# Two decoder layers over a cached grouped-query attention: the first layer's kept heads in another order, a two-head softmax in other steps, and V products issued ahead of scores

## The chip, the cores and the metric

The kernel runs on one core of one Trainium2 chip. The metric is the device time of one execution in microseconds (us), the median of the runs shown. One execution was also taken by the hardware profiler; all lines of profile below come from that one.

## What is computed

Two layers, each an attention block over a long cache and a dense block, one token for each of 8 batches. Both layers read the same caches.

```python
# B=8, one query, D=512, Hq=32, Hkv=8, Sk=8192, Dh=128, F=1792, all bf16
q = (x @ wq) as 32 heads of 128
scores = einsum("bhqd,bhkd->bhqk", q, repeat(k_cache, 4)) * 128**-0.5
o = einsum("bhqk,bhkd->bhqd", softmax(scores), repeat(v_cache, 4)) @ wo

x = x + attention(layernorm(x)); x = x + silu_mlp(layernorm(x))
x = x + attention(layernorm(x)); x = x + silu_mlp(layernorm(x))
```

The K cache and the V cache have 134 MB each, so that two layers that read everything anew would move 537 MB. Four query heads share one K/V head.

## The kernel before

**Tasks and positions.** A task is one layer, batch and K/V head: 128 tasks, in an order that `make_tasks` fixes. A task has 8 positions (`GPT`), two for each of its 4 granules. A granule is 2048 keys of one head: 512 KB, one slot of the ring `ARENA`, which has 28 slots. The build is one loop over positions p; what it emits at each p, in the order of the loop's body, is the order in which every engine runs its part, since each engine runs its list in order.

**Kept heads.** `KEEP = 20` granules, the five heads 3 to 7 of a batch, stay in the ring between the two layers, so that their K is read once for both. Heads 0 to 2 are read twice. V is read in both layers. For each batch the first layer's five kept heads follow each other; then come tasks of heads 0 to 2 of either layer; then the second layer's kept heads. `READ` says how many granules one K load of a kept head brings: 4 for each, a whole head, 2 MB in one transfer. Heads 4 and 5, and 6 and 7 (`DUOS`), are pairs: their rows are interleaved in the ring, they share one softmax, and their V comes in transfers of two granules (1 MB).

**Loads.** `plan_loads` gives each load the position that needs it (`need`), a slot, and the position after which this slot is free (`after`). All loads go through SP's queue in order of `need` (`issue_until`, L394); a load waits there for the last reader of its slot, and those behind it wait too.

**Steps of a task** with first position p0. (1) `emit_t` (L516, DVE): each K granule is transposed in place, one position ahead. (2) `emit_s` (PE): scores. A solo head's granule is L606 with 128 columns, a whole solo head L606 with 512, a whole head of a pair L578 (`score_both`). A whole head in layer one is scored at its last position, p0+7. (3) `softmax`, two tasks later, by phases `p % 8`, for a pair at the positions of its first head's turn: phase 0 maxima (L620, L626 on DVE, L629 on POOL), 2 shift and first exponential (L635 and L638 on DVE, L642 on ACT), 3 first head's transposition on PE (L667) and second exponential, 4 row sums (L655 on DVE for a pair, L652 on ACT for a solo head; then L658 on POOL), 5 last transposition (L667) and copies to `PT` (L674, ACT), 7 reciprocal (L681, DVE). The exponentials use one buffer `P`, so that the second waits for the first one's transposition. (4) `emit_pv` (L711, PE) runs 22 positions (`LP`) behind the scores: a pair's two granules at once, on every fourth position. (5) `emit_own` (L728, ACT), `emit_join` (L736, DVE), `emit_fold` (L750, PE) and `emit_norm` (L760, DVE) bring the head's output into `at`; one position later PE multiplies it by its part of `wo` (L873).

In the loop's body at one position the order is: transposes, scores, V products, own, join, fold, softmax phase, `wo` part or a piece of the dense block's chain, norm, loads.

Of the kernel before, what the change touches and what calls it, by code (L numbers as in the profile page):

```python
# [15 lines left out]
GPT = 8  # L16
GPG = 2
NSLOT = 28
SCORED = 2
READ = (1, 1, 1, 4, 4, 4, 4, 4)  # L20
DUOS = (4, 6)
KEEP = 20
LT = 1
PRE = 10
# [120 lines left out]
class Load:  # L145


    __slots__ = ("kind", "b", "g", "k", "turn", "need", "free", "slot", "after", "wide")

    def __init__(self, kind, b, g, k, need, free, wide=1):  # L150
        self.kind, self.b, self.g, self.k, self.turn = kind, b, g, k, k
        self.need, self.free, self.wide = need, free, wide
        self.slot, self.after = None, None

# [9 lines left out]
def make_tasks(nb, nkv, keep_from):  # L164


    first = int(keep_from)
    a = [[(0, b, g) for g in range(first)] for b in range(nb)]
    kept = [[(0, b, g) for g in range(first, nkv)] for b in range(nb)]
    c = [[(1, b, g) for g in range(first, nkv)] for b in range(nb)]  # L170
    d = [[(1, b, g) for g in range(first)] for b in range(nb)]
    ahead = [t for b in range(1, nb) for t in a[b]]
    behind = []
    tasks = a[0] + kept[0]
    na = gone = 0

    def whole(line, n):
        return n == len(line) or lead_of(line[n][2]) == line[n][2]

    for b in range(nb):  # L180
        if b:
            tasks += kept[b]
        if b == nb - 1:
            nd, nt = len(behind), len(ahead) - na
        else:
            due = 2 * first * (nb - 1) * (b + 1) / nb
            must = first * (b + 1)
# [12 lines left out]


def plan_loads(tasks, kept, nslot, ngran):

    at = {t: i for i, t in enumerate(tasks)}
    loads = []
    for i, (layer, b, g) in enumerate(tasks):
        for k in range(ngran):
            i0 = i * GPT + k * GPG
            if layer == 0 and (g, k) in kept:
                w = READ[g]  # L210
                if k % w == 0:
                    loads.append(Load("K", b, g, k, -1 if i0 < PRE else i0 - LT,
                                      at[(1, b, g)] * GPT + SCORED * GPG + GPG - 1, w))
            elif (g, k) not in kept:
                loads.append(Load("K", b, g, k, -1 if i0 < PRE else i0 - LT, i * GPT + (k + 1) * GPG - 1))
            w = members(g)
            if k % w == 0:
                loads.append(Load("V", b, g, k, i0 + GPG - 1 + LP, i0 + GPG - 1 + LP, w))
    loads.sort(key=lambda d: (d.need, d.kind == "K" and d.wide == 1))
    free = {s: -2 for s in range(nslot)}  # L220
# [42 lines left out]
def _build(ctx, nc, A_x, A_k_cache, A_v_cache, A_wq, A_wo, B_w1, B_w2, out):  # L263
# [43 lines left out]
    def half(slot, h):  # L307
# [29 lines left out]
              "eps": 1, "shift": 1, "eh": FT, "vr": 1, "yr": 1, "tr": 1, "s1": 1, "s1a": 1, "s2": 1, "s2a": 1,  # L337
              "top": DR, "tops": DR, "ssm": DR, "xn": KT // 2, "hs": FT // 2}
    widths.update({f"ssa{n}": DR for n in range(NST)})
    widths.update({f"rs{n}": 2 for n in range(NST)})  # L340
# [69 lines left out]
    t_slot = {}  # L410
    v_slot = {}

    def issue(d):
        cache = A_k_cache if d.kind == "K" else A_v_cache
        own, lead, n = d.g - lead_of(d.g), lead_of(d.g), members(d.g)
        if d.kind == "K":
            rows = cache[d.b, lead:lead + n].rearrange("g (p f) d -> (g p) (f d)", p=128 // n)
            at = own if d.wide > 1 else d.k * n + own
            src = rows[:, at * d.wide * SLOT:(at + 1) * d.wide * SLOT]
        else:  # L420
            src = cache[d.b, d.g].rearrange("(k p c) d -> k p (c d)", k=NGRAN // n, p=128)[d.k // n]
        dst = ARENA[:, d.slot * SLOT:(d.slot + d.wide) * SLOT]
# [6 lines left out]
    with nc.Block() as block:  # L429

        @block.sync
        def _(sync_eng):
# [136 lines left out]

            def score_both(ti, slots, qn):  # L570
                own = tasks[ti][2] - lead_of(tasks[ti][2])
                cols = NGRAN // 2 * 128
                many = ARENA[:, slots[0] * SLOT:(slots[0] + NGRAN) * SLOT].rearrange(
                    "p (k u t x h j e) -> p u t h e k x j", u=2, t=NQ, x=CPB, h=PAIRS, e=2, j=QUAD)
                for u in range(2):
                    bank = (ti - own + u) % NSCP
                    mm_group([
                        lambda n=n, t=t: pe.matmul(  # L578
                            SCp[bank][t * QUAD:t * QUAD + USED, own * cols:(own + 1) * cols], QB[qn][:, n, :],
                            many[:, u, t, n // 2, n % 2], start=(n == 0), stop=(n == NPART - 1))  # L580
                        for n in range(NPART) for t in range(NQ)
                    ], reads=[r_half(slot, h) for slot in slots for h in range(2)] + [f"QB{qn}"], writes=[f"SC{bank}"])

            def emit_s(i):
# [10 lines left out]
                if whole and members(g) > 1:  # L595
                    score_both(ti, slots, qn)
                    return
# [50 lines left out]
            def softmax_sum(ti):  # L648
                st, many = turn_of[ti] % NST, members(tasks[ti][2])
                w = many * REP  # L650
                if many == 1:
                    op(act, lambda: act.activation(ssm[:, 0:w], hm[:, :], ACT.Copy, scale=rs[st][:, 0:1]),  # L652
                       reads=["hm", f"rs{st}"], writes=["ssm"])
                else:
                    op(dve, lambda: dve.scalar_tensor_tensor(  # L655
                        ssm[:, 0:w], rs[st][:, 0:1].to_broadcast([128, w]), rs[st][:, 1:2], hm2, op0=ALU.add, op1=ALU.mult),
                       reads=["hm2", f"rs{st}"], writes=["ssm"])
                op(pool, lambda: pool.partition_all_reduce(ssa[st][:, 0:w], ssm[:, 0:w], 128, bass.bass_isa.ReduceOp.add),  # L658
                   reads=["ssm"], writes=[f"ssa{st}"])
# [19 lines left out]
            def softmax_rcp(ti):  # L679
                st, w = turn_of[ti] % NST, members(tasks[ti][2]) * REP  # L680
                op(dve, lambda: dve.reciprocal(ssa[st][:, 0:w], ssa[st][:, 0:w]), reads=[f"ssa{st}"], writes=[f"ssa{st}"])  # L681

            def softmax(ti, ph):
# [3 lines left out]
                elif ph == 2:  # L687
                    softmax_shift(ti)
                    softmax_exp(ti, 0)
                elif ph == 3 and many > 1:  # L690
                    emit_turn(ti, 0)
                    softmax_exp(ti, 1)
                elif ph == 4:
                    softmax_sum(ti)
                elif ph == 5:
                    emit_turn(ti, many - 1)
                    emit_pt(ti)
                elif ph == 7:
                    softmax_rcp(ti)

            def emit_pv(i):
                ti = i // GPT
                b, g, k, _h = where(i)
                if k % members(g):
                    return
                ob, own, many = ti % 2, g - lead_of(g), members(g)
                lead, at = ti - own, own * NGRAN // many + k // many
                w = XL if ti == ntask - 1 else XW
                parts = [(v_slot[(b, g, k + m)], (lead + m) % NPT) for m in range(many)]
                steps = [  # L710
# [4 lines left out]
                        start=(k == 0 and slot == parts[0][0] and y == 0),  # L715
                        stop=(k + many == NGRAN and slot == parts[-1][0] and y == CPB // w - 1),
                    )
# [35 lines left out]
            def emit_norm(ti):  # L753
                layer, b, g = tasks[ti]
                ob, st, own = ti % 2, turn_of[ti] % NST, g - lead_of(g)
                if layer == 0:
                    dst, rd = at1[b % NAT][:, g * REP:(g + 1) * REP], f"at1_{b % NAT}"
# [339 lines left out]

            kept_from = min(g for g, _k in kept)

            def calm(p):  # L1100
                if p >= NG:
                    return False
                return p >= task_at[(0, turn[0], kept_from)] * GPT

            for p in range(NG + LP + GPT + FOLD + 1):
# [7 lines left out]
                emit_t_until(p + LT)  # L1113
                if p % GPG == GPG - 1 and p < NG:
                    emit_s(p)
                if (p - LP) % GPG == GPG - 1 and 0 <= p - LP < NG:
                    emit_pv(p - LP)
                copied = p - LP - GPT
                if copied >= 0 and copied % GPT == 0 and copied // GPT < ntask:
# [5 lines left out]
                if folded >= 0 and folded % GPT == 0 and folded // GPT < ntask:  # L1125
                    emit_fold(folded // GPT)
                ti = p // GPT - 2
                if 0 <= ti < ntask and lead_of(tasks[ti][2]) == tasks[ti][2]:
                    softmax(ti, p % GPT)
                if chain:  # L1130
# [61 lines left out]
```

## Time and profile before

| what | value |
|---|---|
| median of 3 runs (lowest to highest) | 1168.55 us (1166.8 to 1169.06) |
| profiled execution: its own time, its span | 1169.76 us, 1168.0 us |
| busy: PE, DVE, ACT, POOL | 692.2, 738.9, 315.1, 90.7 us |
| read from memory | 465.05 MB, 398 GB/s over the span |
| mean granted TensorE clock | 0.62 of full speed |
| transposes L516 on DVE | 352, 430.1 us busy, mean 1231 ns |
| maxima L620 on DVE | 128, 86.3 us, mean 674 ns |
| exponentials L642 on ACT | 128, 180.8 us, mean 1413 ns |
| V products L711 on PE | 2064, 259.9 us |
| pair sums L655 on DVE | 32, 7.3 us busy; 88.7 us idle just before them, until ACT's L642 |
| K loads of 2 MB; V loads of 1 MB | 40; 128 |

The span is the time from the first to the last instruction, and the rest of the execution's time lies around it. An idle time belongs to the engine that waited, and the name behind the arrow is what ended the wait. DMA share is the mean busy share of the core's 16 DMA engines. A queue called SPq is SP's sequencer, which issues loads. A pair's task and a solo head's task take the same 8 positions.

### The profile page before, as it was taken

How to read it: one execution, taken by the hardware profiler on the slowest of the kernel's cores; microseconds unless marked ns; L12 is line 12 of the kernel's file. 1: busy time of each engine (PE TensorE's matmuls, PEld its weight loads, DVE VectorE, ACT ScalarE, POOL GpSimd, SP SyncE). 2: the span in 40 equal slices, each digit the busy share in tenths (PEclk: the TensorE clock that was granted, in tenths of full speed). 3: DMA queues.
4: the chain of work that ended last, by engine and by line, in shares of the span. 5: the costliest groups of instructions: out<-in, count | busy, mean ns of one | idle time of the engine just before them, and what ended most of it. 6: DMA issues, size and time to landing. Idle time of an engine off the chain costs nothing.

```text
span 1168.0 us, 28238 instructions
## 1 busy us (share of the span) xinstructions
PE 692.2 (59%) x11792; PEld 377.8 (32%) x11792; DVE 738.9 (63%) x1719; ACT 315.1 (27%) x700; POOL 90.7 (8%) x232
## 2 busy tenths in 40 slices
PE   1525566556665566466665575456765576466676
PEld 1212343234233243133332342234332343133343
DVE  3836655876387664777477655777467664777473
ACT  0342123222322223312222233213322233312322
POOL 0000010001000010001100010001100010001000
PEclk9855565556655575655666577655565555666665
DMA  9999999999999999999999999999999999999993
GB/s 361 404 401 399 408 402 426 417 389 408 401 419 383 399 407 421 422 373 410 412 422 413 395 407 424 420 387 402 412 423 412 391 405 419 423 393 409 412 411 147
DMA packets 94175, 466.90 MB, mean 400 GB/s; under 512 B 9936, under 2 KB 14048, under 8 KB 71904
## 3 DMA queue, kind: packets, MB, share of 16 engines
q1 hardware_dynamic: 94048, 465.10, 98.8%
q8 instruction: 93, 1.52, 0.5%
q14 instruction: 34, 0.28, 0.1%
HBM read 465.05 MB, written 0.01 MB: 398 GB/s over the span
## 4 chain that ended last, share of the span: by engine, by line
DMA 40%; PE 19%; DVE 17%; issue 12%; ACT 6%; SPq 3%; POOL 2%; DVEq 0%; ACTq 0%; POOLq 0%
DMA arena<-in_A_k_cache_dram 33%; DMA arena<-in_A_v_cache_dram 7%; DVE E L736 6%; PE OTp L711 6%; DVE arena L516 4%; ACT E L642 4%; DVE row L620 3%; PE SCp L578 3%; SPq L394 3%; PE TPp L667 2%; PE SCp L606 2%; PE MISC L855 2%; ACT PT L674 1%; PE MISC L873 1%; PE OTp L750 1%
## 5 line engine op out<-in xcount | busy, mean ns | idle before, releaser
L516 DVE STREAM_TRANSPOSE arena<-arena 128x1024 int32<-128x1024 int32 x352 | 430.1, 1231 | 120.0 <-DMA arena<-in_A_k_cache_dram 119.9
L642 ACT ACTIVATE E<-SCp,row 128x512 bf16<-128x512 f32 x128 | 180.8, 1413 | 538.1 <-DVE row L638 463.5
L711 PE MATMUL OTp<-arena,PT 128*16 128x512 bf16 (+1 forms) x2064 | 259.9, 560 | 50.9 <-DMA arena<-in_A_v_cache_dram 31.0
L736 DVE SCALAR_TENSOR_TENSOR E<-OTp,row,E 128x128 f32<-128x128 f32 x381 | 130.4, 342 | 115.3 <-ACT E L728 97.9
L606 PE MATMUL SCp<-arena,QB 128*16 128x128 bf16 (+1 forms) x3328 | 139.3, 314 | 101.6 <-DVE arena L516 87.0
L667 PE MATMUL TPp<-ident,E 128*128 128x128 bf16 x512 | 73.4, 293 | 121.1 <-ACT E L642 120.5
L578 PE MATMUL SCp<-arena,QB 128*16 128x256 bf16 x2048 | 114.0, 389 | 47.1 <-DVE arena L516 30.4
L606 PEld LDWEIGHTS SCp<-arena,QB 128*16 128x16 bf16 x3328 | 70.3, 110 | 173.5 <-DVE arena L516 138.8
L667 PEld LDWEIGHTS TPp<-ident,E 128*128 128x128 bf16 x512 | 41.6, 125 | 185.9 <-ACT E L642 164.2
L750 PE MATMUL OTp<-row,E 128*128 128x4 f32 x254 | 66.4, 332 | 47.3 <-DVE E L736 46.9
L750 PEld LDWEIGHTS OTp<-row,E 128*128 128x128 f32 x254 | 55.4, 272 | 115.6 <-DVE E L736 103.2
L578 PEld LDWEIGHTS SCp<-arena,QB 128*16 128x16 bf16 x2048 | 61.0, 117 | 97.1 <-DVE arena L516 46.1
L629 POOL PARTITION_ALL_REDUCE row<-row x96 | 36.0, 375 | 689.7 <-DVE row L626 575.1
L728 ACT ACTIVATE E<-OTp,row 128x128 f32<-128x128 f32 x127 | 47.4, 373 | 152.4 <-PE OTp L711 152.4
L620 DVE TENSOR_REDUCE row<-SCp 128x1 f32<-128x512 f32 x128 | 86.3, 674 | 2.8
L711 PEld LDWEIGHTS OTp<-arena,PT 128*16 128x16 bf16 (+1 forms) x2064 | 53.5, 107 | 84.7 <-DMA arena<-in_A_v_cache_dram 40.4
L873 PE MATMUL MISC<-at,wo 128*128 128x32 bf16 x1024 | 37.0, 186 | 56.4 <-DVE at L760 55.3
L674 ACT COPY PT<-TPp 128x256 bf16<-128x256 bf16 x128 | 44.3, 372 | 84.6 <-PE TPp L667 84.6
L658 POOL PARTITION_ALL_REDUCE row<-row x96 | 41.3, 431 | 297.5 <-ACT row L652 137.9
L655 DVE SCALAR_TENSOR_TENSOR row<-row 128x8 f32<-128x8 f32 x32 | 7.3, 229 | 88.7 <-ACT E L642 88.7
L873 PEld LDWEIGHTS MISC<-at,wo 128*128 128x128 bf16 x1024 | 32.6, 104 | 65.9 <-DVE at L760 58.8
L563 DVE TENSOR_TENSOR QB<-QSp,row 128x64 bf16<-128x64 f32 (+1 forms) x128 | 24.0, 194 | 15.7 <-PE QSp L547 14.6
(104 smaller groups left out, 385.5 us busy)
## 6 DMA issues: line engine op xcount, KB each, us to landing
arena<-in_A_v_cache_dram SPq DMA_DIRECT2D x256, 512.0 KB, 8.5
arena<-in_A_v_cache_dram SPq DMA_DIRECT2D x128, 1024.0 KB, 12.2
arena<-in_A_k_cache_dram SPq DMA_DIRECT2D x192, 512.0 KB, 8.1
arena<-in_A_k_cache_dram SPq DMA_DIRECT2D x40, 2048.0 KB, 16.1
wq<-in_A_wq_dram SPq DMA_DIRECT2D x1, 4096.0 KB, 17.3
wo<-in_A_wo_dram SPq DMA_DIRECT2D x1, 4096.0 KB, 33.3
w<-in_B_w_dram SPq DMA_DIRECT2D x2, 1792.0 KB, 24.8
E<-in_A_x_dram SPq DMA_DIRECT2D x1, 8.0 KB
```

The source lines that it names most:

```text
L516: op(dve, lambda: dve.transpose(words, words), reads=[r_half(slot, 0), r_half(slot, 1)], writes=[r_half(slot, 0), r_half(slot, 1)])
L578: lambda n=n, t=t: pe.matmul(SCp[bank][t * QUAD:t * QUAD + USED, own * cols:(own + 1) * cols], QB[qn][:, n, :], many[:, u, t, n // 2, n % ...
L606: lambda n=n, t=t: pe.matmul(SCp[bank][t * QUAD:t * QUAD + USED, lo * 128:(lo + len(slots)) * 128], QB[qn][:, n, :], keys(t, n), start=(n ...
L620: op(dve, lambda: dve.tensor_reduce(rowmax[:, n:n + 1], SCp[bank][:, :], AX.X, ALU.max), reads=[f"SC{bank}"], writes=["rowmax"])
L642: op(act, lambda: act.activation(P[:, :].rearrange("p (x j k) -> p k x j", x=CPB, k=NGRAN), SCp[bank][:, :].rearrange("p (k x j) -> p k x ...
L667: lambda c=c: pe.transpose(tpv[:, c, :], P[:, c * 128:(c + 1) * 128], ident[:, :])
L674: op(act, lambda: act.copy(PT[pb][:, :, :, :, :].rearrange("p a t x r -> p x t a r"), tpv.rearrange("p x (t q) -> p x t q", q=QUAD)[:, :, ...
L711: lambda t=t, y=y, slot=slot, pb=pb: pe.matmul(OTp[ob][t * QUAD:t * QUAD + w * REP, 0:w * DH], PT[pb][:, at, t, y * w:(y + 1) * w].rearran ...
L728: op(act, lambda: act.activation(joint, OTp[ob][:, 0:DH], ACT.Copy, scale=own_x[:, 0:1]), reads=[f"OT{ob}", "own_x"], writes=["P"])
L736: op(dve, lambda x=x: dve.scalar_tensor_tensor(joint, OTp[ob][:, x * DH:(x + 1) * DH], own_x[:, x:x + 1], joint, op0=ALU.mult, op1=ALU.add ...
L750: lambda: pe.matmul(OTp[ob][:, 0:REP], joint, hm[:, :], start=True, stop=True)
L873: lambda o=o, h=h: pe.matmul(MISC[:, o * w:(o + 1) * w], wo_sb[:, h, o * 128:(o + 1) * 128], rhs_of(h).to_broadcast([128, w]) if n == 1 el ...
```

## The change

Four edits.

- **Order.** The first layer's kept heads of a batch come as 4, 5, 6, 7, 3, where they came as 3, 4, 5, 6, 7. The second layer's order is as it was.
- **Halves.** `READ[3]` goes from 4 to 2: head 3 is loaded in two transfers of 1 MB and scored in two groups, at its positions 3 and 7.
- **Two-head softmax.** First transposition and second exponential move from phase 3 to 4, last transposition and `PT` copies from 5 to 6 (ahead of `emit_own` there), and the row sums from 4 to 7. One DVE operation on both heads becomes two on ACT, one for each head, POOL sums 16 columns where it summed 8, and DVE adds the two halves. The reciprocal, of solo heads too, is emitted with `emit_norm` of the task's first head, where it was in phase 7.
- **V products first.** At a position at which a kept head is scored, in either layer, the V products go ahead of the scores.

Beside these, `plan_loads` may split a pair's V load in two where fewer than 8 positions (`AMPLE`) lie between `after` and `need`. With this order there is no such load: the plan has 128 V loads of 1 MB and 256 of 512 KB before and after. K loads are 192 of 512 KB, 16 of 1 MB and 32 of 2 MB.

```diff
-READ = (1, 1, 1, 4, 4, 4, 4, 4)
+READ = (1, 1, 1, 2, 4, 4, 4, 4)
+AMPLE = 8
...
-    kept = [[(0, b, g) for g in range(first, nkv)] for b in range(nb)]
+    kept = [[(0, b, g) for g in range(first, nkv) if members(g) > 1] + [(0, b, g) for g in range(first, nkv) if members(g) == 1] for b in range(nb)]
...
 def plan_loads(tasks, kept, nslot, ngran):
+    apart = set()
+    while True:
+        loads = deal(tasks, kept, nslot, ngran, apart)
+        close = {d.key for d in loads if d.kind == "V" and d.wide > 1 and d.need - d.after < AMPLE}
+        if not close:
+            return loads
+        apart |= close
...
             def softmax_sum(ti):
...
-                if many == 1:
-                    op(act, lambda: act.activation(ssm[:, 0:w], hm[:, :], ACT.Copy, scale=rs[st][:, 0:1]),
-                       reads=["hm", f"rs{st}"], writes=["ssm"])
-                else:
-                    op(dve, lambda: dve.scalar_tensor_tensor(
-                        ssm[:, 0:w], rs[st][:, 0:1].to_broadcast([128, w]), rs[st][:, 1:2], hm2, op0=ALU.add, op1=ALU.mult),
-                       reads=["hm2", f"rs{st}"], writes=["ssm"])
-                op(pool, lambda: pool.partition_all_reduce(ssa[st][:, 0:w], ssm[:, 0:w], 128, bass.bass_isa.ReduceOp.add),
+                for n in range(many):
+                    op(act, lambda: act.activation(ssm[:, n * w:(n + 1) * w], masks[many][0], ACT.Copy, scale=rs[st][:, n:n + 1]),
+                       reads=["hm", "hm2", f"rs{st}"], writes=["ssm"])
+                op(pool, lambda: pool.partition_all_reduce(
+                    ssa[st][:, 0:many * w], ssm[:, 0:many * w], 128, bass.bass_isa.ReduceOp.add),
                    reads=["ssm"], writes=[f"ssa{st}"])
...
             def softmax_rcp(ti):
+                if many > 1:
+                    op(dve, lambda: dve.tensor_tensor(ssa[st][:, 0:w], ssa[st][:, 0:w], ssa[st][:, w:2 * w], ALU.add),
+                       reads=[f"ssa{st}"], writes=[f"ssa{st}"])
                 op(dve, lambda: dve.reciprocal(ssa[st][:, 0:w], ssa[st][:, 0:w]), reads=[f"ssa{st}"], writes=[f"ssa{st}"])
...
-                elif ph == 3 and many > 1:
+                elif ph == 4 and many > 1:
                     emit_turn(ti, 0)
                     softmax_exp(ti, 1)
                 elif ph == 4:
                     softmax_sum(ti)
-                elif ph == 5:
+                elif ph == 5 and many == 1 or ph == 6 and many > 1:
                     emit_turn(ti, many - 1)
                     emit_pt(ti)
-                elif ph == 7:
-                    softmax_rcp(ti)
+                elif ph == 7 and many > 1:
+                    softmax_sum(ti)
...
             def emit_norm(ti):
+                if not own:
+                    softmax_rcp(ti)
...
-                if p % GPG == GPG - 1 and p < NG:
+                scored = p % GPG == GPG - 1 and p < NG
+                behind = scored and (tasks[p // GPT][2], p % GPT // GPG) in kept
+                if scored and not behind:
                     emit_s(p)
                 if (p - LP) % GPG == GPG - 1 and 0 <= p - LP < NG:
                     emit_pv(p - LP)
+                if behind:
+                    emit_s(p)
+                probs = p // GPT - 2
+                due_now = 0 <= probs < ntask and lead_of(tasks[probs][2]) == tasks[probs][2]
+                if due_now and p % GPT == 6:
+                    softmax(probs, 6)
```

More of the change, by code (lines that the diff above doesn't have):

```diff
@@ L145 @@
 class Load:
-    __slots__ = ("kind", "b", "g", "k", "turn", "need", "free", "slot", "after", "wide")
+    __slots__ = ("kind", "b", "g", "k", "turn", "need", "free", "slot", "after", "wide", "key")
     def __init__(self, kind, b, g, k, need, free, wide=1):
@@ L152, in __init__ @@
         self.need, self.free, self.wide = need, free, wide
-        self.slot, self.after = None, None
+        self.slot, self.after, self.key = None, None, None
 def lead_of(g):
@@ L202, in plan_loads, with deal @@
 def plan_loads(tasks, kept, nslot, ngran):
+    apart = set()
[5 more added lines that the diff above has]
+        apart |= close
+def deal(tasks, kept, nslot, ngran, apart):
     at = {t: i for i, t in enumerate(tasks)}
@@ L215, in plan_loads @@
                 loads.append(Load("K", b, g, k, -1 if i0 < PRE else i0 - LT, i * GPT + (k + 1) * GPG - 1))
-            w = members(g)
+            key = (layer, b, g, k // members(g))
+            w = 1 if key in apart else members(g)
             if k % w == 0:
                 loads.append(Load("V", b, g, k, i0 + GPG - 1 + LP, i0 + GPG - 1 + LP, w))
+                loads[-1].key = key
     loads.sort(key=lambda d: (d.need, d.kind == "K" and d.wide == 1))
@@ L337, in _build @@
               "eps": 1, "shift": 1, "eh": FT, "vr": 1, "yr": 1, "tr": 1, "s1": 1, "s1a": 1, "s2": 1, "s2a": 1,
-              "top": DR, "tops": DR, "ssm": DR, "xn": KT // 2, "hs": FT // 2}
-    widths.update({f"ssa{n}": DR for n in range(NST)})
+              "top": DR, "tops": DR, "ssm": 2 * DR, "xn": KT // 2, "hs": FT // 2}
+    widths.update({f"ssa{n}": 2 * DR for n in range(NST)})
     widths.update({f"rs{n}": 2 for n in range(NST)})
@@ L411, in _build @@
     v_slot = {}
+    v_wide = {}
     def issue(d):
@@ L417, in issue @@
             rows = cache[d.b, lead:lead + n].rearrange("g (p f) d -> (g p) (f d)", p=128 // n)
-            at = own if d.wide > 1 else d.k * n + own
+            at = (own * NGRAN + d.k) // d.wide if d.wide > 1 else d.k * n + own
             src = rows[:, at * d.wide * SLOT:(at + 1) * d.wide * SLOT]
         else:
-            src = cache[d.b, d.g].rearrange("(k p c) d -> k p (c d)", k=NGRAN // n, p=128)[d.k // n]
+            rows = cache[d.b, d.g].rearrange("(k p c) d -> k p (c d)", k=NGRAN // n, p=128)[d.k // n]
+            src = rows[:, d.k % n * SLOT:(d.k % n + d.wide) * SLOT]
+            v_wide[(d.b, d.g, d.k)] = d.wide
         dst = ARENA[:, d.slot * SLOT:(d.slot + d.wide) * SLOT]
@@ L568, in emit_q, with score_both @@
                        reads=["QS", "own_q"], writes=[f"QB{n}"])
-            def score_both(ti, slots, qn):
+            def score_both(ti, slots, qn, first):
                 own = tasks[ti][2] - lead_of(tasks[ti][2])
-                cols = NGRAN // 2 * 128
-                many = ARENA[:, slots[0] * SLOT:(slots[0] + NGRAN) * SLOT].rearrange(
+                lo = (own * NGRAN + first) // 2 * 128
+                hi = lo + len(slots) // 2 * 128
+                many = ARENA[:, slots[0] * SLOT:(slots[0] + len(slots)) * SLOT].rearrange(
                     "p (k u t x h j e) -> p u t h e k x j", u=2, t=NQ, x=CPB, h=PAIRS, e=2, j=QUAD)
@@ L578, in score_both @@
                         lambda n=n, t=t: pe.matmul(
-                            SCp[bank][t * QUAD:t * QUAD + USED, own * cols:(own + 1) * cols], QB[qn][:, n, :],
+                            SCp[bank][t * QUAD:t * QUAD + USED, lo:hi], QB[qn][:, n, :],
                             many[:, u, t, n // 2, n % 2], start=(n == 0), stop=(n == NPART - 1))
@@ L595, in emit_s @@
                 if whole and members(g) > 1:
-                    score_both(ti, slots, qn)
+                    score_both(ti, slots, qn, first)
                     return
@@ L679, in softmax_rcp @@
             def softmax_rcp(ti):
-                st, w = turn_of[ti] % NST, members(tasks[ti][2]) * REP
+                st, many = turn_of[ti] % NST, members(tasks[ti][2])
+                w = many * REP
+                if many > 1:
+                    op(dve, lambda: dve.tensor_tensor(ssa[st][:, 0:w], ssa[st][:, 0:w], ssa[st][:, w:2 * w], ALU.add),
+                       reads=[f"ssa{st}"], writes=[f"ssa{st}"])
                 op(dve, lambda: dve.reciprocal(ssa[st][:, 0:w], ssa[st][:, 0:w]), reads=[f"ssa{st}"], writes=[f"ssa{st}"])
@@ L703, in emit_pv @@
                 b, g, k, _h = where(i)
-                if k % members(g):
+                if v_wide.get((b, g, k - k % members(g)), 1) > 1 and k % members(g):
                     return
@@ L708, in emit_pv @@
                 w = XL if ti == ntask - 1 else XW
-                parts = [(v_slot[(b, g, k + m)], (lead + m) % NPT) for m in range(many)]
+                parts = [(v_slot[(b, g, k + m)], (lead + (k + m) % many) % NPT) for m in range(v_wide[(b, g, k)])]
                 steps = [
@@ L715, in emit_pv @@
                         start=(k == 0 and slot == parts[0][0] and y == 0),
-                        stop=(k + many == NGRAN and slot == parts[-1][0] and y == CPB // w - 1),
+                        stop=(k + len(parts) == NGRAN and slot == parts[-1][0] and y == CPB // w - 1),
                     )
@@ L1096, in _ @@
             due_of = {t: p for p, t in due.items()}
-            kept_from = min(g for g, _k in kept)
+            kept_heads = {g for g, _k in kept}
             def calm(p):
@@ L1102, in calm @@
                     return False
-                return p >= task_at[(0, turn[0], kept_from)] * GPT
+                return p >= min(task_at[(0, turn[0], g)] for g in kept_heads) * GPT
             for p in range(NG + LP + GPT + FOLD + 1):
@@ L1126, in _ @@
                     emit_fold(folded // GPT)
-                ti = p // GPT - 2
-                if 0 <= ti < ntask and lead_of(tasks[ti][2]) == tasks[ti][2]:
-                    softmax(ti, p % GPT)
+                if due_now and p % GPT != 6:
+                    softmax(probs, p % GPT)
                 if chain:
```

## The prediction

> **What bounds the kernel now.** I read the page's DMA rows and chain first, then busy time by windows, then the timeline around one dip.
>
> ```profile
> DMA  9999999999999999999999999999999999999993
> q1 hardware_dynamic: 94048, 465.10, 98.8%
> DMA 40%; PE 19%; DVE 17%; issue 12%; ACT 6%; SPq 3%; POOL 2%; DVEq 0%; ACTq 0%; POOLq 0%
> ```
>
> The DMA engines are busy for 98.8% of the span, DVE for 63%. The change moves the same 465 MB, so only pauses of the DMA stream can be won. Where they are (columns: stretch, length, busy time of PE, PEld, DVE, ACT, POOL, granted clock, DMA share, GB/s):
>
> ```profile
> 420.00:500.00 80.00, 48.25 (x728) 24.58 (x720) 47.36 (x122) 23.89 (x49) 6.39 (x16) 0.65 1.02 418
> 260.00:290.00 30.00, 20.88 (x490) 13.83 (x491) 21.50 (x56) 8.97 (x28) 4.01 (x10) 0.57 1.03 408
> 499.80:514.80 15.00, 9.47 (x156) 4.86 (x148) 12.29 (x23) 2.60 (x4) 0.37 (x1) 0.61 0.96 362
> 514.80:529.80 15.00, 7.93 (x142) 3.97 (x142) 9.50 (x17) 1.89 (x6) 0.40 (x1) 0.50 1.00 385
> ```
>
> 418 and 408 GB/s are an unbroken stream of large and of small loads. In the 30 us after head 7's K has landed (499.8 us in batch 3) it falls to 362 and 385. The same view for the eight batches gives, for the two stretches of 15 us: 399+386, 394+386, 375+375, 362+385, 404+384, 387+387, 386+389, 401+391. Against 410, each loses 15 x (2 - sum/410): 1.3, 1.5, 2.6, 2.7, 1.2, 1.7, 1.7, 1.0, together 13.5 us. That is nearly all that this change can reach: 1.7 us a batch.
>
> Why the stream thins out, in batch 3 (start, duration, engine, line; in brackets the idle time before and what ended it):
>
> ```profile
> 499.81 1.25 DVE L516 STREAM_TRANSPOSE arena<-arena 128x1024 int32<-128x1024 int32 x1 [1.86 <-DMA arena<-in_A_k_cache_dram]
> 505.79 1.89 PE L578 MATMUL SCp<-arena,QB 128*16 128x256 bf16 x32 [1.01 <-DVE arena L516]
> 506.09 1.25 DVE L516 STREAM_TRANSPOSE arena<-arena 128x1024 int32<-128x1024 int32 x1 [0.35 <-DMA arena<-in_A_k_cache_dram]
> 507.26 1.08 DVE L736 SCALAR_TENSOR_TENSOR E<-OTp,row,E 128x128 f32<-128x128 f32 x3
> 508.26 1.47 DVE L620 TENSOR_REDUCE row<-SCp 128x1 f32<-128x512 f32 x2
> 509.04 3.96 SPq L394 DMA_DIRECT2D arena<-in_A_k_cache_dram  x2
> 511.26 0.12 DVE L760 TENSOR_TENSOR at<-OTp,row 128x4 bf16<-128x4 f32 x1
> 511.75 1.44 ACT L642 ACTIVATE E<-SCp,row 128x512 bf16<-128x512 f32 x1 [6.56 <-DVE row L638]
> 513.37 0.61 PE L667 MATMUL TPp<-ident,E 128*128 128x128 bf16 x4
> 515.44 0.23 DVE L655 SCALAR_TENSOR_TENSOR row<-row 128x8 f32<-128x8 f32 x1 [2.64 <-ACT E L642]
> 517.40 1.07 PE L711 MATMUL OTp<-arena,PT 128*16 128x512 bf16 x8
> 518.56 0.33 SPq L394 DMA_DIRECT2D arena<-in_A_v_cache_dram  x1
> 522.29 1.25 DVE L516 STREAM_TRANSPOSE arena<-arena 128x1024 int32<-128x1024 int32 x1 [1.94 <-DMA arena<-in_A_k_cache_dram]
> 527.67 1.25 DVE L516 STREAM_TRANSPOSE arena<-arena 128x1024 int32<-128x1024 int32 x1 [2.52 <-DMA arena<-in_A_k_cache_dram]
> ```
>
> Call T the landing of head 7 (499.8) and a unit 512 KB, which takes 1.25 us in an unbroken stream (506.09 is unit 5: 6.29/5). Four transposes and the score take T to T+7.9; maxima at T+8.5; exponentials, transpositions and copies bring the V product of head 6 at T+17.6, and only then is its slot free for head 7's V, issued T+18.8. The rows at 522.29 and 527.67 are units 17 and 21 of the stream: due 521.05 and 526.05, so 1.2 and 1.6 us late. Two issues came too late: one at 512.7 (the second of the row at 509.04, which waits for the second granule's score behind the `wo` part and L760) and the one at 518.56.
>
> **The change, part by part.** In both plans 20 units lie from head 7's K through head 7's V, the last of them freed by head 6's V product: the loop is as long as it was. What changes is what runs inside it.
>
> *Order and V first.* Before, the loads that went out only after T+8 were units 11 to 20; after, the plan frees the slots of units 5 to 12 before T+1 those of 13 to 16 by V products at T+3.6 and T+6.1, no longer behind head 7's score (1.9 us), and those of 17 and 18 by one at T+15. So the issue at T+12.9 and its followers are no longer late. Gain: at most the 1.2 us that unit 17 was late, 8 x 1.2 = 9.6 us.
>
> *The pair's chain gets longer.* Head 3's first half now stands where the single granule of 506.09 stood: its transpose is ahead of the join (L736) and the maxima on DVE, and 1 MB lands at unit 6 (T+7.5), not 5. Transpose 1.25 and join 1.08 put the maxima at T+9.8, 1.3 later. Then reciprocal (L681, 0.19) and the new add (as L623, 0.16) stand ahead of L760: +0.35, and the `wo` part waits for L760 as before. Behind it PE has the V product (1.06) and now a score of 2 granules (16 of L578's 32: 0.94, where L606 took 0.4 here) ahead of the transposition: +0.55. Against that, head 6's V product no longer waits for a granule's score, held up by the sum at 515.44: -0.64 (517.40 against `PT` ready at 516.76). Sum +1.6: head 7's V, issued at T+18.8 before, is issued at T+20.4; added up operation by operation from the maxima on it comes to T+20.7. I take T+20.6.
>
> *What that costs.* Unit 18 ends at T+22.5, so this issue has 1.9 us of stream ahead of it. How early a load must be issued I bound from both sides by the trace's DMA records: a V load issued at 296.03 landed 3.4 us later (2.1 of start, 1.25 of data); a K load issued at 512.67 landed at 518.13, 5.5 us (4.2 of start). So unit 20 is 0.2 to 2.3 us late; I take 0.75, V loads being nearest to the first row. The next two K granules, issued behind the second half's score and the `wo` part at T+22.1 and T+24.0, come out 0.3 and 0.7 late by a start of 3.9, the V behind them 0.2: 1.95 a batch. Bounds 0.4 (the low ends) and 3.2 (the high ends added). Against 1.7 now: +0.25 x 8 = +2 us, from -10 to +12.
>
> *The late sums* take DVE out of the 88.7 us in which it waited for ACT (32 times 2.8). Half are in the second layer, and in the first layer's first pairs, where the stream runs at 418: hidden, gain 0. The last pair's 2.64 is counted above. Two ACT copies (L652, 0.3 each) for one L655 lie in ACT's idle 73%; POOL's sum costs 0.43 whether 4 or 8 wide. If ACT's cover were gone, 0.6 x 16 = 10 us.
>
> *The reciprocal* moves 0.17 to 0.19 of DVE time in front of L760, so every `wo` part waits 0.2 longer. Loads among small granules are issued 4 to 7 us ahead, so 0; exposed once a batch, 1.6.
>
> *V first in the second layer* lets the first kept head's score, which frees four slots at once, wait 0.6 for a V product. In batch 1 the loads freed there were already late (0.2 and 1.0 in the DMA records), in the other seven not: +0.5; all eight exposed, 5.
>
> *Halves.* Eight more transfers in 616, same bytes. Small loads run at 408 and large at 418, 2.4%; 16 MB of head 3 is 40 us, and halves are still of the large kind: 0 to 1.0, taken 0.4. The Trainium skill ("DMA: Bandwidth & Descriptors", section "Anatomy of one DMA") gives each transfer a fixed 2.0 us beside its bytes (fitted there on transfers that GpSimd issued). Paid in the stream by each of the eight, that would be an estimated +16 us by that page. The trace disagrees that it is paid there: 512 KB loads, by the page 3.2 us each, pass at 408 GB/s, one each 1.28 us, because several are in flight.
>
> **Sum.** +2.0 +0.5 +0.4 = +2.9 us on the profiled execution's 1169.8 (span 1168.0 and 1.8 around it): 1172.7. The median is 1.2 below that execution, so 1171.5.
>
> **Rivals.**
> *The dips fill up (faster).* If a V load needs 2.1 us or less and the chain of the pair is not lengthened (DVE takes the join before the half has landed, or PE has its transposition at once), unit 20 is on time and what is left is 0.4 a batch: 8 x (0.4 - 1.7) = -10.4, 1158. For it: at T the queue holds 12 units, where it held 6. Against: 20 units of loop either way. It decides from an issue of head 7's V before T+19.
> *New waits in the stream of small granules (slower).* Reciprocal in front of L760, V product in front of the second layer's score, PE's in-order list: 1.6 + 5, with the high bound of the dip for half the batches (4 x 1.3 = 5): 1168.5 + 12 = 1180. Against: the small loads' 408 has 4 us of lead.
> *Nothing that counts.* The splitting of V loads never comes into play, sums and order are hidden: 1168 to 1169. For it: DMA at 98.8%.
>
> **Chances.** The forecast (the stall moves from the issue at T+13 to the one at T+20) 0.46, own range 1166 to 1177; dips filled 0.27; new waits 0.17; nothing 0.10. A measurement here tells 0.2% (2.3 us) from no change. Faster by more: 0.03 of the forecast, 0.25 of the filled dips, 0.02 of the last, 0.30. Within: 0.14, 0.02, 0.07: 0.23. Slower: 0.29, 0.17, 0.01: 0.47. The range takes in most of the filled dips and of the new waits: 1159 to 1181.
>
> **What would show it.** In the 30 us after head 7 lands: no late issue near T+13, the pair's maxima near T+9.8, head 7's V issued near T+20.6, then K granules' transposes waiting for DMA near T+25 to T+30; GB/s by 15 us first near 405, then lower, in the second stretch or third. No wait of DVE for ACT before the sums. Wrong if head 7's V is issued by T+19, if the two stretches reach 405 both, or if small-granule stretches fall below 408.

## The result, and the profile after

| | before | changed |
|---|---|---|
| median of 4 runs each | 1167.80 us | 1175.70 us |
| lowest to highest | 1166.80 to 1169.06 us | 1174.99 to 1177.74 us |
| ratio to before, 95% interval | | 1.0066 [1.0051, 1.0081] |
| profiled execution, its span | 1169.76, 1168.0 us | 1174.99, 1173.3 us |
| mean granted TensorE clock | 0.62 | 0.61 |

The changed kernel is 7.9 us (0.66%) slower. In the code after, transposes are L533, a pair's maxima L638, exponentials L660, the add of the sums L698, the reciprocal L700, a pair's V products L730, join L755, norm L781, the `wo` part L894, loads L408.

The page of the changed kernel, its DMA row, its DMA queue and its chain of waits:

```profile
DMA  9999999999999999999999999999999999999993
q1 hardware_dynamic: 95200, 465.10, 98.4%
DMA 30%; DVE 22%; PE 22%; issue 14%; ACT 8%; POOL 2%; SPq 1%; DVEq 0%; ACTq 0%; POOLq 0%
```

The same 465.10 MB, with the DMA engines 98.4% busy where they were 98.8%. The chain runs less through DMA (30%, it was 40%) and more through DVE and PE. That fits a stream that is held up more often by work that frees slots late; the timeline below shows where.

Busy time by windows around head 7's K in batch 3, which now lands at 488.8 us (T); the columns are stretch, length, busy time of PE, PEld, DVE, ACT, POOL, granted clock, DMA share, GB/s:

```profile
488.80:503.80 15.00, 8.51 (x124) 4.28 (x128) 12.98 (x26) 3.10 (x8) 0.83 (x2) 0.61 1.01 419
503.80:518.80 15.00, 9.50 (x164) 5.19 (x156) 9.69 (x15) 3.29 (x10) 0.46 (x1) 0.61 0.91 346
518.80:533.80 15.00, 8.29 (x164) 4.61 (x163) 10.74 (x24) 4.13 (x8) 1.63 (x4) 0.61 1.01 404
```

The first stretch is now an unbroken stream (before: 362), the second falls to 346 (before: 385). All eight batches show it: the first stretch has 416 to 422, the second 338 to 376 (mean 354). By the prediction's own formula the two together lose 15 x (2 - (418.1 + 354.3)/410) = 1.7 us a batch, as before. The dip has moved by 15 us and has not become smaller.

The timeline of those 30 us (start, duration, engine, line; in brackets the idle time before and what ended it):

```profile
488.81 1.25 DVE L533 STREAM_TRANSPOSE arena<-arena 128x1024 int32<-128x1024 int32 x1 [2.06 <-DMA arena<-in_A_k_cache_dram]
493.82 0.80 SPq L408 DMA_DIRECT2D arena<-in_A_k_cache_dram  x2
496.26 1.25 DVE L533 STREAM_TRANSPOSE arena<-arena 128x1024 int32<-128x1024 int32 x1 [0.89 <-DMA arena<-in_A_k_cache_dram]
497.43 1.08 DVE L755 SCALAR_TENSOR_TENSOR E<-OTp,row,E 128x128 f32<-128x128 f32 x3
498.43 1.48 DVE L638 TENSOR_REDUCE row<-SCp 128x1 f32<-128x512 f32 x2
501.44 0.12 DVE L698 TENSOR_TENSOR row<-row 128x8 f32<-128x8 f32 x1
501.60 0.20 DVE L700 RECIPROCAL row<-row 128x8 f32<-128x8 f32 x1
501.91 0.16 DVE L781 TENSOR_TENSOR at<-OTp,row 128x4 bf16<-128x4 f32 x1
502.13 0.61 PE L894 MATMUL MISC<-at,wo 128*128 128x32 bf16 x16 [2.97 <-DVE at L781]
502.44 1.48 ACT L660 ACTIVATE E<-SCp,row 128x512 bf16<-128x512 f32 x1 [8.29 <-DVE row L656]
503.80 0.80 SPq L408 DMA_DIRECT2D arena<-in_A_k_cache_dram  x2
508.02 1.03 PE L730 MATMUL OTp<-arena,PT 128*16 128x512 bf16 x8 [0.83 <-ACT PT L689]
509.14 0.33 SPq L408 DMA_DIRECT2D arena<-in_A_v_cache_dram  x1
510.42 2.25 SPq L408 DMA_DIRECT2D arena<-in_A_k_cache_dram  x2
516.14 1.25 DVE L533 STREAM_TRANSPOSE arena<-arena 128x1024 int32<-128x1024 int32 x1 [2.67 <-DMA arena<-in_A_k_cache_dram]
525.46 1.25 DVE L533 STREAM_TRANSPOSE arena<-arena 128x1024 int32<-128x1024 int32 x1 [1.40 <-DMA arena<-in_A_k_cache_dram]
```

Head 3's first half is transposed at 496.26, ahead of the join and the maxima (T+9.6). Add, reciprocal and norm stand in a row at 501.44 to 502.07, and both the `wo` part and the first exponential come behind them. Head 7's V is issued at 509.14, T+20.3, the K granules behind it from 510.42 on. At 516.14 a transpose has waited 2.67 us for its K: T+27.3.

What became of the sums' wait on DVE, first before, then after (columns: the line that waited, what it waited for, us in total, times, longest):

```profile
DVE E L736 <- ACT E L728: 97.9, 35, 4.4
DVE row L655 <- ACT E L642: 88.7, 32, 3.7
```
```profile
DVE E L755 <- ACT E L747: 156.0, 56, 6.3
```

The wait of 88.7 us before the sums is gone, and the join's wait for its own copy has grown by 156.0 - 97.9 = 58.1 us. In ACT's list that copy stands behind the second exponential and the copies to `PT`, before the change and after it; DVE, no longer held at the sums, comes to the join earlier and waits there for the same chain. Two thirds of the freed time is another wait.

### The profile page after: what moved, and what is told of

Read it like the earlier page. It is cut to its first block, busy times and chain, and to the rows that moved or that the text cites. A ratio compares the mean times of both kernels' runs of the same rounds, so it can differ in the third digit from the quotient of the medians.

```text
span 1173.3 us, 28634 instructions
## 1 busy us (share of the span) xinstructions
PE 689.5 (59%) x11920; PEld 383.4 (33%) x11920; DVE 749.7 (64%) x1719; ACT 331.2 (28%) x764; POOL 92.6 (8%) x232
## 3 DMA queue, kind: packets, MB, share of 16 engines
q1 hardware_dynamic: 95200, 465.10, 98.4%
## 4 chain that ended last, share of the span: by engine, by line
DMA 30%; DVE 22%; PE 22%; issue 14%; ACT 8%; POOL 2%; SPq 1%; DVEq 0%; ACTq 0%; POOLq 0%
DMA arena<-in_A_k_cache_dram 27%; DVE arena L533 7%; DVE E L755 6%; PE OTp L730 6%; ACT E L660 5%; PE SCp L596 4%; PE TPp L682 4%; DVE row L638 4%; DMA arena<-in_A_v_cache_dram 4%; PE SCp L624 3%; PE MISC L876 2%; PE OTp L769 2%; ACT PT L689 2%; DVE row L644 1%; SPq L408 1%
## 5 line engine op out<-in xcount | busy, mean ns | idle before, releaser
L533 DVE STREAM_TRANSPOSE arena<-arena 128x1024 int32<-128x1024 int32 x352 | 430.8, 1233 | 129.2 <-DMA arena<-in_A_k_cache_dram 128.7
L660 ACT ACTIVATE E<-SCp,row 128x512 bf16<-128x512 f32 x128 | 181.5, 1418 | 562.3 <-DVE row L656 483.3
L730 PE MATMUL OTp<-arena,PT 128*16 128x512 bf16 (+1 forms) x2064 | 255.9, 564 | 67.1 <-DMA arena<-in_A_v_cache_dram 27.5
L755 DVE SCALAR_TENSOR_TENSOR E<-OTp,row,E 128x128 f32<-128x128 f32 x381 | 130.9, 344 | 169.3 <-ACT E L747 156.0
L624 PE MATMUL SCp<-arena,QB 128*16 128x128 bf16 (+2 forms) x3456 | 137.4, 306 | 91.8 <-DVE arena L533 82.5
L624 PEld LDWEIGHTS SCp<-arena,QB 128*16 128x16 bf16 x3456 | 76.6, 111 | 163.4 <-DVE arena L533 126.0
L596 PEld LDWEIGHTS SCp<-arena,QB 128*16 128x16 bf16 x2048 | 66.0, 120 | 86.6 <-issue 36.4
L638 DVE TENSOR_REDUCE row<-SCp 128x1 f32<-128x512 f32 x128 | 87.4, 683 | 3.3
L730 PEld LDWEIGHTS OTp<-arena,PT 128*16 128x16 bf16 (+1 forms) x2064 | 47.3, 102 | 101.1 <-issue 60.0
L894 PE MATMUL MISC<-at,wo 128*128 128x32 bf16 x1024 | 36.8, 185 | 70.8 <-DVE at L781 59.2
L894 PEld LDWEIGHTS MISC<-at,wo 128*128 128x128 bf16 x1024 | 31.7, 102 | 79.2 <-DVE at L781 74.3
L670 ACT ACTIVATE row<-row 128x8 f32<-128x8 f32 (+1 forms) x128 | 38.6, 302 | 2.6
L580 DVE TENSOR_TENSOR QB<-QSp,row 128x32 bf16<-128x32 f32 (+1 forms) x128 | 23.5, 189 | 18.4 <-PE QSp L564 17.3
```

What stands on the lines that cost most here:

```text
L533: op(dve, lambda: dve.transpose(words, words), reads=[r_half(slot, 0), r_half(slot, 1)], writes=[r_half(slot, 0), r_half(slot, 1)])
L596: lambda n=n, t=t: pe.matmul(SCp[bank][t * QUAD:t * QUAD + USED, lo:hi], QB[qn][:, n, :], many[:, u, t, n // 2, n % 2], start=(n == 0), st ...
L624: lambda n=n, t=t: pe.matmul(SCp[bank][t * QUAD:t * QUAD + USED, lo * 128:(lo + len(slots)) * 128], QB[qn][:, n, :], keys(t, n), start=(n ...
L638: op(dve, lambda: dve.tensor_reduce(rowmax[:, n:n + 1], SCp[bank][:, :], AX.X, ALU.max), reads=[f"SC{bank}"], writes=["rowmax"])
L660: op(act, lambda: act.activation(P[:, :].rearrange("p (x j k) -> p k x j", x=CPB, k=NGRAN), SCp[bank][:, :].rearrange("p (k x j) -> p k x ...
L730: lambda t=t, y=y, slot=slot, pb=pb: pe.matmul(OTp[ob][t * QUAD:t * QUAD + w * REP, 0:w * DH], PT[pb][:, at, t, y * w:(y + 1) * w].rearran ...
```

## Experiments

Each kernel was timed against the kernel before on the same chip; ratios carry 95% intervals. Unless said otherwise an experiment is the changed kernel with the edit shown.

### How long may the chain be? Head 3 in quarters, in halves, whole

```diff
-READ = (1, 1, 1, 2, 4, 4, 4, 4)
+READ = (1, 1, 1, 1, 4, 4, 4, 4)      # e3_quarters
+READ = (1, 1, 1, 4, 4, 4, 4, 4)      # e4_whole
```

> The changed kernel with head 3 read and scored by granules of 512 KB (same slots, same positions after which slots are free). Theory: the first transpose of head 3 ends 1.25 us earlier and the score ahead of the pair's first transposition is 0.4 instead of 0.94, so the maxima stand at T+8.5 and head 7's V is issued near T+18.9: 8 x 1.3 or more less than the changed kernel, 1165 us (1161 to 1168). Rival (the size of head 3's transfers has no part in it): 1174 to 1177.

> The changed kernel with head 3 read whole (2 MB), same slots. Theory: head 3 lands at T+10, the join and the maxima on DVE stand behind its transpose, maxima near T+12.3, head 7's V issued near T+22.2, 1.6 us later than with halves: 1188 us (1181 to 1193). Rival (size of transfers has no part): 1174 to 1177.

Quarters: 1163.12 us, 0.9951 [0.9933, 0.9968]. Whole: 1196.86 us, 1.0246 [1.0219, 1.0273], 9 us more than expected. The second stretch of 15 us behind T in batch 3, quarters, then whole (columns as in the windows above):

```profile
499.60:514.60 15.00, 9.38 (x164) 5.01 (x162) 9.47 (x16) 3.18 (x8) 0.47 (x1) 0.50 0.96 376
```
```profile
512.40:527.40 15.00, 8.92 (x154) 4.29 (x154) 9.94 (x19) 4.63 (x10) 0.46 (x1) 0.68 0.78 265
```

376, 346 and 265 GB/s for a first transfer of 0.5, 1 and 2 MB: the longer head 3's first piece takes to land, the later the pair's maxima behind its transposes, and the deeper the dip. The maxima start at T+9.3, T+9.8 and T+12.2, head 7's V goes out at T+19.3, T+20.4 and T+22.4 (means of seven batches, from the starts in the trace; in the first batch a load of weights lies among these loads, so it is left out). For quarters T+8.5 and T+18.9 had been expected.

`READ` changes two things at once, the piece that lands and the piece that is scored. Of the 1.1 us between quarters and halves, 0.5 lie ahead of the maxima and the rest behind them, where PE's score ahead of the pair's first transposition is 0.64 us for one granule and 1.07 for two (batch 3). No run here has one without the other.

### Old order, new order

```diff
-READ = (1, 1, 1, 2, 4, 4, 4, 4)
+READ = (1, 1, 1, 4, 4, 4, 4, 4)
-    kept = [[(0, b, g) ... if members(g) > 1] + [(0, b, g) ... if members(g) == 1] for b in range(nb)]
+    kept = [[(0, b, g) for g in range(first, nkv)] for b in range(nb)]      # e1_oldorder
```

> Late sums, moved reciprocal and V products first, but heads 3 to 7 in the old order and head 3 whole. Theory (the order with halves lengthens the chain from head 7's K to head 6's V product): the chain is nearly that of the kernel before, head 7's V issued T+18.9, so 1168 us (1166 to 1170), about 7 below the changed kernel. Rival (the softmax steps, the reciprocal ahead of the norm and V first cost the time): 1174 to 1177, as the changed kernel.

`e2_orderonly` is the complement: the new order with halves, the softmax of before (sums on DVE in phase 4, reciprocal in phase 7), scores ahead of V.

> New order with head 3 in halves alone; softmax steps and the order of V products and scores as before. Theory: the chain is the longest of all, since DVE waits for the second exponential ahead of the half's transposes and head 6's V product stands behind the half's score: head 7's V issued near T+21.5, 1180 us (1176 to 1186). Rival (the other edits cost the time): 1167 to 1170.

Old order with the other edits: 1172.72 us, 1.0029 [1.0014, 1.0045]. That is neither the 1168 us of the theory nor the 1174 to 1177 of the rival: the other edits do cost something. Order and halves alone: 1176.96 us, 1.0067 [1.0047, 1.0088], at the low end of what was expected. Alone, order and halves make it 0.67% slower, the rest 0.29%; together 0.66%. The edits do not add, so something in one makes up for the other.

### The other edits in the old order

`e5_vfirst_only` is the kernel before with V products first alone, `e6_sums_only` the kernel before with the two-head softmax alone.

> The kernel before with V products first alone. Theory (of the edits beside the order it is the reciprocal and the add, 0.35 us ahead of the norm and so of the wo part and of the next score, that cost): no change, 1168 us (1166 to 1170); head 6's V is issued near T+6.4, where it was T+8.8. Rival (V products first costs, by holding back scores that free K slots): 1171 to 1174.

> The kernel before with the late sums, later phases and the reciprocal beside the norm alone. Theory: the load that was issued at T+12.9 goes out 0.5 later, at T+13.4, and the stream loses 0.3 to 0.5 a batch: 1171 us (1169.5 to 1174). Rival (V products first is what costs): 1167 to 1169.

V first: 1170.99 us, 1.0017 [0.9998, 1.0035], not told from nothing. The softmax: 1178.60 us, 1.0085 [1.0066, 1.0104]. The prediction had put it at nothing and this run's expectation at 3 us; it costs more than the whole change.

The old order with both, e1, stands at 1.0029, and it differs from e6 by V first alone (each against the kernel before on its own chip). So beside a softmax that costs 0.85%, V first gives back 0.56% (6.5 us), where alone it gives nothing. This is one place where the edits do not add.

The softmax edit moves the sums, the phases and the reciprocal, so the reciprocal was put back:

```diff
             def emit_norm(ti):
-                if not own:
-                    softmax_rcp(ti)
...
             def emit_own(ti):
+                if lead_of(tasks[ti][2]) == tasks[ti][2]:
+                    softmax_rcp(ti)
```

This is `e10_sums_rcpown` on e6, `e7_rcpown` on the changed kernel, and `e8_q_rcpown` on e3. Add and reciprocal are the same two operations, only issued three positions earlier, with the head's own copy (`emit_own`).

> The old order of heads, scores of whole heads ahead of V, late row sums (as in e6_sums_only, which took 1178.6 us), and the reciprocal and the add issued with the head's own part instead of with the norm. Theory A (in e6 it was the reciprocal and the add ahead of the norm that made the load of head 8's first half of K late): 1168 us (1166 to 1171), that load issued back near T+12.9. Rival B (it is the later phases of the pair's transposes and copies): it stays at 1175 to 1179, the load near T+13.4.

> The changed kernel (head 3 in halves) with one edit: the reciprocal and the add of the two halves of the row sums are issued together with the head's own part, two steps of the softmax earlier, and not with the norm. Theory A (the reciprocal ahead of the norm delays wo and the score behind it, and with it every later load's issue; with head 3 in quarters the same edit gave 4.5 us): 1171 us (1169 to 1173), head 7's V issued near T+20.0 in place of T+20.4. Rival B (in halves the score of two granules decides, the reciprocal is hidden behind it): unchanged, 1174 to 1177.

> Head 3 by granules, and reciprocal and add emitted with the own copy, two positions earlier, where DVE waits for a load. Theory: maxima to first exponential 3.5 us again (4.0 in the changed kernel), head 7's V 0.4 us earlier than with granules alone: 8 x 0.3, 1161 us (1158 to 1163). Rival (the place of the reciprocal has no part): 1163 to 1164.5.

| kernel | reciprocal with the norm | reciprocal early |
|---|---|---|
| old order, late sums | 1.0085 [1.0066, 1.0104] | 0.9980 [0.9963, 0.9998] |
| the change (halves) | 1.0066 [1.0051, 1.0081] | 0.9990 [0.9971, 1.0009] |
| quarters | 0.9951 [0.9933, 0.9968] | 0.9917 [0.9896, 0.9939] |

The early reciprocal gives 1.05%, 0.76% and 0.34%: 12, 9 and 4 us. The medians were 1167.63, 1168.77 and 1158.62 us. In the old order the whole loss of e6 goes; in halves the gain is larger than the 3 to 7 us of theory A. The timeline of e6, then of e10, around the issue at T+13 (T is 501.5 and 500.3):

```profile
510.98 4.23 SPq L408 DMA_DIRECT2D arena<-in_A_k_cache_dram  x2
...
513.14 0.20 DVE L700 RECIPROCAL row<-row 128x8 f32<-128x8 f32 x1
513.45 0.16 DVE L781 TENSOR_TENSOR at<-OTp,row 128x4 bf16<-128x4 f32 x1
...
513.67 0.59 PE L894 MATMUL MISC<-at,wo 128*128 128x32 bf16 x16 [2.56 <-DVE at L781]
```
```profile
506.29 0.20 DVE L700 RECIPROCAL row<-row 128x8 f32<-128x8 f32 x1
...
509.51 3.78 SPq L408 DMA_DIRECT2D arena<-in_A_k_cache_dram  x2
...
511.78 0.12 DVE L781 TENSOR_TENSOR at<-OTp,row 128x4 bf16<-128x4 f32 x1
...
511.96 0.57 PE L894 MATMUL MISC<-at,wo 128*128 128x32 bf16 x16 [2.07 <-DVE at L781]
```

In e6 the `wo` part starts at T+12.2 and the last issue of the SP row (its end less 0.33) is at T+13.4; in e10 T+11.7 and T+12.7. Half a microsecond on DVE has become 0.5 on PE and 0.7 at the load, in this batch; as a mean of seven batches that load is issued at T+13.3 in e6 and at T+12.8 in e10.

The changed kernel with the early reciprocal (e7), same places as in the timeline of the changed kernel (T = 488.1):

```profile
500.72 0.12 DVE L781 TENSOR_TENSOR at<-OTp,row 128x4 bf16<-128x4 f32 x1
...
500.90 0.61 PE L894 MATMUL MISC<-at,wo 128*128 128x32 bf16 x16 [2.47 <-DVE at L781]
501.21 1.47 ACT L660 ACTIVATE E<-SCp,row 128x512 bf16<-128x512 f32 x1 [8.24 <-DVE row L656]
...
502.56 0.80 SPq L408 DMA_DIRECT2D arena<-in_A_k_cache_dram  x2
...
507.91 0.33 SPq L408 DMA_DIRECT2D arena<-in_A_v_cache_dram  x1
```

`wo` at T+12.8 (it was T+13.3), exponential T+13.1 (13.6), K loads T+14.5 (15.0), head 7's V T+19.8 (20.3): everything behind the norm is 0.5 us earlier. Who held up the `wo` part, over the whole run, in the changed kernel, then in e7 (us, times):

```profile
  DVE at L781: 133.4, 75
```
```profile
  DVE at L781: 117.6, 79
```

### Are the late sums worth anything?

`e9_q_rcpown_ph35` is e8 with the pair's transpositions and copies back in phases 3 and 5, a position ahead of the join's copy. `e11_q_oldsums` is e3 with the softmax of before.

> As the one before, and a pair's transpositions, second exponential and copies in phases 3 and 5 again; the row sums stay in phase 7. Theory: the own copy is no longer behind the PT copies, so DVE's wait for it falls from 145 us to about 100, and with the sums late no other wait takes its place; the scores of granules after the pair's come earlier: 1160 us (1157 to 1163). Rival (these waits lie beside the stream): as the one before, within 1 us.

> Head 3 read in quarters, new order of heads, V ahead of scores of whole heads, and the softmax as it was before the change (the sum of a pair made by VectorE right behind its exponentials, the reciprocal at the end of the same task). Compare e8 (1158.6 us, the same with late sums and an early reciprocal) and e3 (1163.1 us, the same with late sums and the reciprocal ahead of the norm). Theory A (the VectorE waits that late sums remove lie beside the load stream, so they are worth nothing): 1159 us (1157 to 1161). Rival B (the freed VectorE time is worth something once nothing else is late): 1162 to 1166.

e9: 1158.95 us, 0.9918 [0.9896, 0.9940]. e11: 1159.07 us, 0.9910 [0.9887, 0.9933]. Both equal e8. The waits of DVE for ACT in e8, e9 and e11:

```profile
DVE E L757 <- ACT E L749: 133.0, 44, 6.2
```
```profile
DVE E L757 <- ACT E L749: 132.4, 45, 6.2
```
```profile
DVE E L755 <- ACT E L747: 92.5, 36, 4.0
DVE row L673 <- ACT E L660: 89.2, 32, 3.7
```

In e9 the join's wait was expected to fall to about 100 us, and it did not fall: the phases have no part in it. It is the early sums of e11 that make it short, and then DVE waits 89.2 us ahead of the sums. Both waits together are 49 us longer in e11 than in e8 at the same time, so these waits lie beside the stream.

### Is V first worth anything?

```diff
-                behind = scored and (tasks[p // GPT][2], p % GPT // GPG) in kept
+                behind = False      # e12_q_noV, on e8
```

> As e8 (head 3 in quarters, new order, late sums, early reciprocal: 1158.6 us), but with scores of whole heads ahead of V products as before the change. It asks whether V first does anything. In halves, e2 (scores first, softmax as before the change) issued head 7's V at T+20.8 and took 1.0067 of before; e7 (V first, late sums, early reciprocal) issued it at T+19.9 and took 0.999; late sums alone were worth nothing in e10 and e11. Theory A (V first is what lies between e2 and e7, 0.9 us a batch at head 7's V): here the issue moves from T+18.5 to about T+19.4, as in e3, and the time to 1163 us (1161 to 1166), 0.995 of before. Rival B (in quarters a V product has room enough; V first is worth nothing, as in the old order, where it made 1.0017): 1158 to 1160, 0.991 to 0.993.

1159.75 us, 0.9919 [0.9902, 0.9936], with head 7's V at T+18.4: rival B. V first is worth nothing here, where no reciprocal stands in front of the norm; in the old order with one there it was worth 0.56% (e1 against e6). In halves it was not tried alone: what lies between e2 (1.0067) and e7 (0.9990), V first or the late sums, stays open.

### Time against the issue of head 7's V

All kernels with the new order, by the mean issue of head 7's V behind T (seven batches, from the SP rows of the trace):

| kernel | issue | ratio to before |
|---|---|---|
| e11, e12, e8, e9 (quarters, no reciprocal at the norm) | T+18.2, 18.4, 18.5, 18.7 | 0.9910, 0.9919, 0.9917, 0.9918 |
| e3 (quarters, reciprocal at the norm) | T+19.3 | 0.9951 |
| e7 (halves, reciprocal early) | T+19.9 | 0.9990 |
| the change | T+20.4 | 1.0066 |
| e2 (halves, scores first, softmax of before) | T+20.8 | 1.0067 |
| e4 (whole) | T+22.4 | 1.0246 |

Below T+18.7 the ratio no longer moves. From there to T+22.4 it rises by 0.033, which is 38 us over 3.7 us of delay and 8 batches: 1.3 us of time for each us of delay in a batch. The K granules behind that load, whose slots are freed behind the same chain, are late with it: in batch 3 of the change that V lands 0.3 us late, the two K behind it 1.1 and 1.4. The mean granted clock over a kernel's runs is 0.62 to 0.63 for every kernel of this table, so it does not tell them apart. What the stream looks like when nothing is late (e8, T = 483.5, windows as above):

```profile
483.50:498.50 15.00, 9.71 (x168) 5.12 (x168) 13.72 (x26) 3.56 (x9) 0.83 (x2) 0.73 1.02 413
498.50:513.50 15.00, 7.68 (x152) 4.04 (x144) 9.29 (x18) 2.86 (x8) 0.46 (x1) 0.61 1.00 393
513.50:528.50 15.00, 8.90 (x163) 4.80 (x163) 11.00 (x21) 4.78 (x10) 1.62 (x4) 0.50 1.02 408
```

413, 393 and 408 GB/s, where the change had 419, 346 and 404. The four fastest kernels take about 1159 us, 0.8 to 0.9% under the kernel before. All have the new order and quarters, and none has the reciprocal in front of the norm.

## Why the prediction was right, and where it was not

**What bounds it: right.** The stream bounds the kernel, and the 30 us behind head 7's K are where it is won or lost. Nine kernels with the same bytes and the new order span 1159 to 1197 us, in step with that one issue.

**Order and V first: the late issue moved, as forecast.** K loads go out at T+5.0 and T+15.0 with the first stretch full (419; the prediction said near 405). The gain was real in place and given back in the second stretch. That V first would do part of it is not borne out in quarters: e12 lacks it and loses nothing. What it does in halves is open.

**The pair's chain: right in place and size.** Forecast maxima T+9.8, head 7's V T+20.6, K transposes waiting near T+25 to T+30. Measured (means) T+9.8 and T+20.4, the transpose at T+27.3.

**What that costs: right, step by step.** Forecast for the changed kernel: head 7's V 0.75 us late, the two K granules behind it 1.05 and 1.75, the V behind them 1.95. By the landings of the loads (means of seven batches, late against 1.25 us for each unit of 512 KB behind T) they are 0.8, 1.4, 1.6 and 1.8 us late; before the change the same units were 1.6 to 1.8 late. At the 36th unit it is 2.9 us after and 2.7 before: +0.24 a batch, in all +1.9 of the +2.0 forecast.

**The late sums: right at 0, as far as tried.** e10 shows it in the old order, e11 beside e8 and e9 in quarters; in halves they were not tried alone. That 58.1 of the 88.7 us would come back as the join's wait was not foreseen, and costs nothing.

**The reciprocal: this is the term that was mis-sized.** "Loads among small granules are issued 4 to 7 us ahead, so 0; exposed once a batch, 1.6" is what the prediction said of it, and +0.35 us of delay inside the pair's chain, which it priced only as a whole. Add and reciprocal take 0.5 us there (501.44 to 501.91), and taken away from the norm they give back 1.0066 - 0.9990, about 9 us, more than the change lost. By the landings the 36th unit is then 2.3 us late and not 2.9: 0.65 us a batch, so that 5 of the 9 us lie in the dips. In the profiled executions of the change and of e7, 7.7 us apart, another 2.1 lie behind the last load and 0.4 in the rest of the stream. The small granules' stretch from T+31 to T+61 in batch 1 runs at 410 GB/s (before: 408). So the 0 among small granules is not contradicted; the price lies in the chain, where the term was never set apart.

**Halves: right to be small as a transfer.** The eight extra transfers were priced at +0.4. The price of the halves is the chain's: quarters, with 16 more transfers than halves, are 1.2% faster. The Trainium skill ("DMA: Bandwidth & Descriptors", section "Anatomy of one DMA") gives each transfer a fixed 2.0 us, fitted there on transfers that GpSimd issued: for the 16 more an estimate of +32 us, if paid in the stream. The runs speak against paying it there.

**The sum.** Forecast +2.9 for the profiled pair; the spans give 1173.3 - 1168.0 = +5.3. Beside the dips' 1.9 there are 1.5 us behind the last load (it lands 18.0 us before the end, before 16.5; 0.8 of that is the output's transfer, 2.5 against 1.7), for which the prediction had no term, and 1.9 in the rest of the stream. There it had +0.5 for V first in the second layer and +0.4 for halves; one pair of executions does not put the 1.9 down to a single cause, and no run shows these two terms apart. The medians lie 7.9 apart because the profiled execution of before was 2.0 us above its median and that of after 0.7 below; the prediction had taken 1.2 above for both. So the sum was 2.4 short, and the step from profile to median 1.9.

**Rivals.** "The dips fill up" gave 1158 and an issue before T+19 as its point of decision: that is what quarters with an early reciprocal do, at 1158.6. The change as made stood 1.4 us beyond that point. "New waits" named the reciprocal in front of L760, at 1.6 in all. It named the right operation, but among the small granules, where the runs show little; its price, 9 us in all and 5 of them in the dips, was several times higher. That the time came out inside the range owes something to the range's width, 1159 to 1181, which took in most of three different accounts.

## What to carry to other kernels

On a kernel bound by its load stream, look for the instruction that frees the slot for the next load, and count every operation ahead of it, however short: two DVE operations of 0.1 and 0.2 us in front of a norm cost 9 us here, and issued three positions earlier they cost nothing that the runs tell. Where a chain of dependent work begins with a landing, try to read and score that piece in small transfers; here the smallest that was tried, 512 KB, was the best. A wait of 90 us on an engine that is 63% busy can be worth nothing, so find what the stream waits for before removing it.

## What was not expected

Head 3 in transfers of 512 KB beats it in 1 and 2 MB by 1.2% and 3.0%, though small loads move at 408 GB/s in this kernel and large ones at 418. The same kernel before, over all chips and runs of this study, took from 1165.78 to 1175.07 us, so that changes of 0.3% were told only by ratios on one chip.
